# A gated state-space and GELU layer on one core: table GELU, one pool of PSUM banks and a new order of stages

## The chip, the core and the metric

The kernel runs on one core of a Trainium2 chip. The engines are TensorE (PE in the profile; PEld is its weight load), VectorE (DVE), ScalarE (ACT), GpSimd (POOL) and SyncE (SP), which issues most of the loads and stores. Matmul results land in a memory called PSUM, which these kernels use as eight banks of 512 f32 columns for each partition. The time is device time in microseconds (us). A profile of one execution has its own span, which is about 2 us shorter than that execution's time.

## The reference

Tokens are 2048, the width D is 640, the state has 640 entries, the hidden width F is 1728. For each token

```python
g = sigmoid((x * gate_w).sum(-1))
a = 2 * Re(h @ C.T) + x * Dskip      # h[t] = Lam_bar * h[t-1] + B_bar x[t], complex
b = gelu_tanh(x @ w1 + b1) @ w2 + b2
out = g * a + (1 - g) * b            # bf16
```

Both kernels turn the complex recurrence into a real one. They rotate the input by a table of cosines and sines, run a real scan with decay `r` on DVE, and rotate back. The work comes in stages over chunks of tokens: **ff1** (x times w1, then GELU), **ssm** (x times B, rotation, scan, rotation), **fin_b** (GELU output times w2, scaled by 1 - g into `gb`) and **fin_a** (states times C, plus the skip; `ot` = g times this plus `gb`, then the store).

## The kernel before

Chunks are 512, 512, 512, 384 and 128 tokens. A scheduler fixes each engine's order of instructions before the run; as the traces below show, it is not always the order of the program.

```python
CHUNKS = [512, 512, 512, 384, 128]
# start: x by a transposing DMA, then w1 in two parts (896 and 832 columns)
nc.sync.dma_start_transpose(out=xT[:, :, 0:Q], in_=x2d[0:Q, :])
nc.sync.dma_start(out=w1_sb[:, :, 0:FH], in_=B_w1[:, 0:FH].rearrange(...))
# ... (cut) tables TSIN, TCOS: seven DVE and two ACT passes per 128 states
ps1 = tile_pool(name="ps1", bufs=2, space=PSUM)   # ps_h and ps_bu: two banks each
ps2 = tile_pool(name="ps2", bufs=1, space=PSUM)   # psA and psB: two banks each, one buffer

def gelu_unit(c, kf):
    # ... (cut) five matmuls into ps_h
    nc.scalar.activation(out=xb, in_=ps_h, func=ACT.Identity, bias=b1_c)
    nc.scalar.activation(out=x2k, in_=ps_h, func=ACT.Square, bias=sb1_c, scale=SQRT_GELU_K)
    nc.scalar.activation(out=tpl, in_=x2k, func=ACT.Identity, bias=1.0)
    nc.vector.tensor_tensor(out=upl, in0=tpl, in1=xb, op=ALU.mult)
    nc.scalar.activation(out=sg, in_=upl, func=ACT.Sigmoid, scale=GELU_2C)
    nc.vector.tensor_tensor(out=gt, in0=xb, in1=sg, op=ALU.mult)

def final_B(ti):
    # ... (cut) 14 x (512 + 128) columns into psB, five gate matmuls into psB[:, 640:641]
    nc.scalar.activation(out=gcol[:, 0:1], in_=psB[:, 640:641], func=ACT.Sigmoid)
    nc.scalar.activation(out=gcol[:, 1:2], in_=psB[:, 640:641], func=ACT.Sigmoid, scale=-1.0)
    nc.scalar.activation(out=gb, in_=psB[:, 0:D], func=ACT.Identity, scale=gcol[:, 1:2])

def final_A(ti):
    # ... (cut) 10 x (512 + 128) columns and five diag matmuls into psA
    nc.vector.scalar_tensor_tensor(out=ot, in0=psA[:, 0:D], scalar=gcols[ti][:, 0:1], in1=gbs[ti], ...)
    nc.sync.dma_start(out=out2d[tcols, :], in_=ot)

# ... (cut) chunk 0, ctilde() (scales C by the input factors on DVE), then
for c in range(1, NCH):          # simplified: the last chunk differs a little
    for ks in range(KS):
        ssm_unit(c, ks)
        for kf in groups[ks]:
            gelu_unit(c, kf)
    carry_batch(c)
    for ti in tiles_of(c - 1):
        final_B(ti)
        final_A(ti)
```

Of the kernel before, what the change touches and what calls it, by code (L numbers as in the profile page):

```python
# [10 lines left out]
ALU = mybir.AluOpType  # L11
# [5 lines left out]
P = 128  # L17
T = 2048
D = 640
NS = 640  # L20
F = 1728
CH = 512
CHUNKS = [512, 512, 512, 384, 128]
NCH = len(CHUNKS)
CH_OFF = [sum(CHUNKS[:i]) for i in range(NCH)]
KD = D // P
KS = NS // P
KF = (F + P - 1) // P
F_LAST = F - (KF - 1) * P
NT = T // P  # L30

MAGIC = 12582912.0
TWO_PI_M = float(np.float32(2.0 * np.pi * (1.0 - 2.0 ** -20)))
INV_2PI = float(np.float32(1.0 / (2.0 * np.pi)))
GELU_K = 0.044715
SQRT_GELU_K = float(np.sqrt(GELU_K))
GELU_2C = float(2.0 * np.sqrt(2.0 / np.pi))
# [3 lines left out]
def kernel(  # L41
# [18 lines left out]
    dbg: dict | None = None,  # L60
):
    nc = tc.nc
    if dbg is None:
        dbg = {}

    def dbg_out(key, ap_sb):
        if key in dbg:
            nc.sync.dma_start(out=dbg[key], in_=ap_sb)

# [3 lines left out]
    const = ctx.enter_context(tc.tile_pool(name="const", bufs=1))  # L73
    hsp = ctx.enter_context(tc.tile_pool(name="hsp", bufs=2))
    gelp = ctx.enter_context(tc.tile_pool(name="gelp", bufs=2))

    xT = const.tile([P, KD, T], BF16, name="xT")
    w1_sb = const.tile([P, KD, F], BF16, name="w1_sb")
    w2_sb = const.tile([P, KF, D], BF16, name="w2_sb")
    BT_re = const.tile([P, KD, NS], BF16, name="BT_re")  # L80
    BT_im = const.tile([P, KD, NS], BF16, name="BT_im")
    CCA = const.tile([P, KS, D], BF16, name="CCA")
    CCB = const.tile([P, KS, D], BF16, name="CCB")
    TCOS = const.tile([P, KS, CH], BF16, name="TCOS")
    TSIN = const.tile([P, KS, CH], BF16, name="TSIN")

    praw = const.tile([P, 4, KS], BF16, name="praw")
    pf32 = const.tile([P, 4, KS], F32, name="pf32")
    lre_c = pf32[:, 0, :]
    lim_c = pf32[:, 1, :]  # L90
    ldt_c = pf32[:, 2, :]
    dsk_c = pf32[:, 3, :]
    b1raw = const.tile([P, KF], BF16, name="b1raw")
    b1_c = const.tile([P, KF], F32, name="b1_c")
    gw_c = const.tile([P, KD], BF16, name="gw_c")
    ident = const.tile([P, P], BF16, name="ident")
    diag = const.tile([P, KD, P], BF16, name="diag")
    tf = const.tile([P, CH], F32, name="tf")
    carry = const.tile([P, KS, 4], F32, name="carry")
    ends = const.tile([P, 2, KS], F32, name="ends")  # L100

    with nc.allow_non_contiguous_dma(reason="small parameter loads"):
        nc.scalar.dma_start(out=praw[:, 2, :], in_=A_log_dt.rearrange("(j p) -> p j", p=P))
        nc.scalar.dma_start(out=praw[:, 1, :], in_=A_Lambda_im.rearrange("(j p) -> p j", p=P))
        nc.scalar.dma_start(out=praw[:, 0, :], in_=A_Lambda_re.rearrange("(j p) -> p j", p=P))
        nc.scalar.dma_start(out=b1raw[:, 0:KF - 1], in_=B_b1[0:(KF - 1) * P].rearrange("(j p) -> p j", p=P))
        nc.scalar.dma_start(out=b1raw[:F_LAST, KF - 1:KF], in_=B_b1[(KF - 1) * P:F].rearrange("(j p) -> p j", p=F_LAST))
    Q = CH
    nc.sync.dma_start_transpose(out=xT[:, :, 0:Q], in_=x2d[0:Q, :])
    FH = 7 * P  # L110
    nc.sync.dma_start(out=w1_sb[:, :, 0:FH], in_=B_w1[:, 0:FH].rearrange("(kd p) f -> p kd f", p=P))
    nc.sync.dma_start(out=w1_sb[:, :, FH:F], in_=B_w1[:, FH:F].rearrange("(kd p) f -> p kd f", p=P))
    nc.sync.dma_start_transpose(out=BT_re[:, :, :], in_=A_B_re[:, :])  # L113
    nc.sync.dma_start_transpose(out=BT_im[:, :, :], in_=A_B_im[:, :])
    nc.sync.dma_start_transpose(out=xT[:, :, Q:2 * Q], in_=x2d[Q:2 * Q, :])

    smallp_cm = tc.tile_pool(name="smallp", bufs=1)
    smallp = smallp_cm.__enter__()

    def col(name, dtype=F32, n=KS):  # L120
        return smallp.tile([P, n], dtype, name=name)

    nc.vector.tensor_copy(out=pf32[:, 0:3, :], in_=praw[:, 0:3, :])
    nc.vector.memset(b1_c[:], 0.0)
    nc.vector.tensor_copy(out=b1_c[:, 0:KF - 1], in_=b1raw[:, 0:KF - 1])
    nc.vector.tensor_copy(out=b1_c[:F_LAST, KF - 1:KF], in_=b1raw[:F_LAST, KF - 1:KF])
# [4 lines left out]
    nc.vector.tensor_copy(out=dt32[:], in_=dt16[:])  # L131
    dtl = col("dtl")
# [3 lines left out]
    th_c = col("th_c")  # L136
    nc.vector.tensor_tensor(out=th_c[:], in0=dt32[:], in1=lim_c, op=ALU.mult)
    thp_c = const.tile([P, KS], F32, name="thp_c")
    nc.vector.tensor_scalar(out=thp_c[:], in0=th_c[:], scalar1=INV_2PI, scalar2=None, op0=ALU.mult)

    def sincos_cols(w_ap, sin_out, cos_out, tagp):
        kq = col(tagp + "_kq")
        nc.vector.tensor_scalar(out=kq[:], in0=w_ap, scalar1=MAGIC, scalar2=MAGIC, op0=ALU.add, op1=ALU.subtract)
        red = col(tagp + "_red")
        nc.vector.tensor_tensor(out=red[:], in0=w_ap, in1=kq[:], op=ALU.subtract)
        nc.scalar.activation(out=sin_out, in_=red[:], func=ACT.Sin, scale=TWO_PI_M)
        wq = col(tagp + "_wq")
        nc.vector.tensor_scalar(out=wq[:], in0=w_ap, scalar1=0.25, scalar2=None, op0=ALU.add)
        kcq = col(tagp + "_kcq")
        nc.vector.tensor_scalar(out=kcq[:], in0=wq[:], scalar1=MAGIC, scalar2=MAGIC, op0=ALU.add, op1=ALU.subtract)  # L150
        redc = col(tagp + "_redc")
        nc.vector.tensor_tensor(out=redc[:], in0=wq[:], in1=kcq[:], op=ALU.subtract)
        nc.scalar.activation(out=cos_out, in_=redc[:], func=ACT.Sin, scale=TWO_PI_M)

    sth = col("sth"); cth = col("cth")
    sincos_cols(thp_c[:], sth[:], cth[:], "t1")
    rot = {}
    for L in sorted(set(CHUNKS[:-1])):
        wL = col(f"w{L}")
        nc.vector.tensor_scalar(out=wL[:], in0=thp_c[:], scalar1=float(L), scalar2=None, op0=ALU.mult)  # L160
        sL = const.tile([P, KS], F32, name=f"s{L}")
        cL = const.tile([P, KS], F32, name=f"c{L}")
        sincos_cols(wL[:], sL[:], cL[:], f"t{L}")
        nsL = const.tile([P, KS], F32, name=f"ns{L}")
        nc.vector.tensor_scalar(out=nsL[:], in0=sL[:], scalar1=-1.0, scalar2=None, op0=ALU.mult)
        rot[L] = (cL, sL, nsL)

    a_c = col("a_c"); b_c = col("b_c")
    nc.vector.tensor_tensor(out=a_c[:], in0=r_c[:], in1=cth[:], op=ALU.mult)
    nc.vector.tensor_tensor(out=b_c[:], in0=r_c[:], in1=sth[:], op=ALU.mult)  # L170
# [8 lines left out]
    cre = col("cre"); cim = col("cim"); t2c = col("t2c")  # L179
# [5 lines left out]
    nc.vector.tensor_tensor(out=t2c[:], in0=am1[:], in1=lim_c, op=ALU.mult)  # L185
    nc.vector.tensor_tensor(out=cim[:], in0=cim[:], in1=t2c[:], op=ALU.subtract)
    nc.vector.tensor_tensor(out=cim[:], in0=cim[:], in1=rden[:], op=ALU.mult)
    c2re = const.tile([P, KS], F32, name="c2re")
    m2ci = const.tile([P, KS], F32, name="m2ci")
    m2cr = const.tile([P, KS], F32, name="m2cr")  # L190
    nc.vector.tensor_scalar(out=c2re[:], in0=cre[:], scalar1=2.0, scalar2=None, op0=ALU.mult)
    nc.vector.tensor_scalar(out=m2ci[:], in0=cim[:], scalar1=-2.0, scalar2=None, op0=ALU.mult)
    nc.vector.tensor_scalar(out=m2cr[:], in0=cre[:], scalar1=-2.0, scalar2=None, op0=ALU.mult)

    sb1_c = const.tile([P, KF], F32, name="sb1_c")
    nc.vector.tensor_scalar(out=sb1_c[:], in0=b1_c[:], scalar1=SQRT_GELU_K, scalar2=None, op0=ALU.mult)
    make_identity(nc, ident[:])
    iot = smallp.tile([P, CH], I32, name="iot")
    nc.gpsimd.iota(iot[:], pattern=[[1, CH]], base=0, channel_multiplier=0)
    nc.vector.tensor_copy(out=tf[:], in_=iot[:])  # L200
    smallp_cm.__exit__(None, None, None)

    with tc.tile_pool(name="tabw", bufs=1) as tabw:
        for ks in range(KS):
            w = tabw.tile([P, CH], F32, name="w")
            nc.vector.tensor_scalar(out=w[:], in0=tf[:], scalar1=thp_c[:, ks:ks + 1], scalar2=None, op0=ALU.mult)
            kk = tabw.tile([P, CH], F32, name="kk")
            nc.vector.tensor_scalar(out=kk[:], in0=w[:], scalar1=MAGIC, scalar2=MAGIC, op0=ALU.add, op1=ALU.subtract)
            red = tabw.tile([P, CH], F32, name="red")
            nc.vector.tensor_tensor(out=red[:], in0=w[:], in1=kk[:], op=ALU.subtract)  # L210
            nc.scalar.activation(out=TSIN[:, ks, :], in_=red[:], func=ACT.Sin, scale=TWO_PI_M)
            wq = tabw.tile([P, CH], F32, name="wq")
            nc.vector.tensor_scalar(out=wq[:], in0=w[:], scalar1=0.25, scalar2=None, op0=ALU.add)
            kc = tabw.tile([P, CH], F32, name="kc")
            nc.vector.tensor_scalar(out=kc[:], in0=wq[:], scalar1=MAGIC, scalar2=MAGIC, op0=ALU.add, op1=ALU.subtract)
            redc = tabw.tile([P, CH], F32, name="redc")
# [44 lines left out]
    def ssm_unit(c, ks):  # L261
# [14 lines left out]
        if c == 0 and ks == 0:  # L276
            dbg_out('bu16', bu16[:])
# [205 lines left out]
```

## Time and profile before

| | before |
|---|---|
| time, first measurement | 277.16 us (276.76 to 279.09) |
| span | 275.5 us |
| PE busy | 228.8 us, 83% |
| DVE busy | 215.1 us, 78% |
| ACT busy | 183.2 us, 66% |
| PE idle | 275.5 - 228.85 = 46.7 us |

These lines are from the page of the kernel before: part 1 (busy time, share, instructions) and part 2 (busy tenths in 40 slices of 6.9 us; PEclk is the granted clock in tenths).

```profile
PE 228.8 (83%) x1528; PEld 120.5 (44%) x1528; DVE 215.1 (78%) x545; ACT 183.2 (66%) x401; POOL 3.3 (1%) x12
...
PE   0357058897979888999888989998988999999994
...
DVE  0399989999999999998999989119998921699111
ACT  0369989888936788847888984139999621895111
...
PEclk9999658999999999999999999999999999999999
```

No engine is full over the span: PE has 83%, DVE 78% and ACT 66%. The next lines are from the groups of instructions by form; the columns are busy time, mean ns of one, and idle time of the engine just before, with what ended it.

```profile
L339 ACT ACTIVATE xb<-ps_h,b_c 128x512 bf16<-128x512 f32 x39 | 26.8, 687 | 1.2 <-DVE gel L349 0.7 <-PE ps_h L331 0.5
L341 ACT ACTIVATE x2k<-ps_h,sb_c 128x512 bf16<-128x512 f32 x39 | 26.7, 685 | 0.0
L344 ACT ACTIVATE tpl<-x2k 128x512 bf16<-128x512 bf16 x39 | 24.5, 629 | 0.0
...
L348 ACT ACTIVATE sg<-upl 128x512 bf16<-128x512 bf16 x39 | 23.8, 627 | 15.9 <-DVE upl L346 15.9
...
L349 DVE TENSOR_TENSOR gel<-xb,sg 128x512 bf16<-128x512 bf16 x39 | 15.8, 410 | 0.2
...
L346 DVE TENSOR_TENSOR upl<-tpl,xb 128x512 bf16<-128x512 bf16 x39 | 15.4, 405 | 1.3 <-ACT tpl L344 1.3
```

The GELU of one 128x512 unit is four ACT passes, 2.63 us in all, and two DVE passes, while its five matmuls need 5 x 0.215 us. The waits of the kernel before (in total, times, longest):

```profile
PE ps_h L331 <- ACT x2k L341: 25.8, 23, 9.5
...
PE ps_h L331 <- DMA w_sb<-in_B_w_dram: 11.3, 1, 11.3
```

The table of stages gives, for each stretch of the span, its length, the busy time of PE, PEld, DVE, ACT and POOL with the number of instructions, the granted clock, the DMA share and GB/s:

```profile
0.00:20.00 20.00, 6.58 (x18) 2.19 (x19) 8.77 (x56) 6.47 (x16) 2.20 (x9) 1.00 0.98 226
20.00:40.00 20.00, 7.85 (x29) 3.08 (x29) 18.87 (x47) 18.86 (x31) 0.00 (x0) 0.74 1.03 213
40.00:80.00 40.00, 36.12 (x163) 15.46 (x162) 40.00 (x80) 33.55 (x61) 0.00 (x0) 0.96 0.11 40
80.00:120.00 40.00, 34.15 (x229) 17.65 (x228) 40.00 (x87) 29.63 (x57) 0.00 (x0) 1.00 0.03 9
120.00:275.50 155.50, 144.14 (x1094) 82.14 (x1092) 107.50 (x279) 94.69 (x238) 1.13 (x3) 1.00 0.04 16
```

Of the 46.7 us in which PE is idle, 13.4 fall before 20 us (the first matmul waits 11.3 us for w1), 12.2 from 20 to 40 us, 9.7 from 40 to 120 us and 11.4 after. From 40 to 120 us DVE has no pause at all. At the start and after the wait of 9.5 us, PE's weight loads are 0.43 us apart (11.3 to 15.1 us and 37.8 to 41.6 us) where they are 0.22 us apart later: matmuls at half rate.

### The profile page before, as it was taken

The page shows a single profiled execution, that of the slowest core. Times are in us where ns is not written, and L with a number is a line of the kernel's source. Part 1 is how long each engine was busy: PE and PEld are TensorE (multiplying, and loading weights), DVE is VectorE, ACT ScalarE, POOL GpSimd, SP SyncE. Part 2 cuts the span into 40 slices and gives each one's busy share as a digit, 9 for nine tenths or more (in the row PEclk, how much of TensorE's full clock was granted, in tenths as well). Part 3 has the DMA queues.
Part 4 walks back from the last instruction along what each step waited for, and adds up shares of the span by engine and source line. Part 5 has one row for each costly group of instructions (what it writes and reads, how often), then busy time and mean ns, then how long its engine had stood idle before and what let it go on. Part 6 is the DMA issues. An engine that isn't in the chain of part 4 may idle for free.

```text
span 275.5 us, 4172 instructions
## 1 busy us (share of the span) xinstructions
PE 228.8 (83%) x1528; PEld 120.5 (44%) x1528; DVE 215.1 (78%) x545; ACT 183.2 (66%) x401; POOL 3.3 (1%) x12
## 2 busy tenths in 40 slices
PE   0357058897979888999888989998988999999994
PEld 0113023343434444554333445555444555766552
DVE  0399989999999999998999989119998921699111
ACT  0369989888936788847888984139999621895111
POOL 3000000000000000000000000000000000000000
PEclk9999658999999999999999999999999999999999
DMA  7999994000000000000000000100000000000000
GB/s 101 335 231 214 219 245 157 2 0 1 0 0 2 0 24 26 1 26 24 1 0 0 2 12 14 48 24 2 0 2 2 24 26 24 26 0 26 24 27 24
DMA packets 33702, 13.22 MB, mean 48 GB/s; under 512 B 28625, under 2 KB 33682, under 8 KB 33682
## 3 DMA queue, kind: packets, MB, share of 16 engines
q1 hardware_dynamic: 29954, 12.95, 18.0%
q10 hardware_dynamic: 3728, 0.01, 0.7%
q8 instruction: 12, 0.20, 0.3%
q14 instruction: 8, 0.07, 0.1%
HBM read 4.43 MB, written 2.62 MB: 26 GB/s over the span
## 4 chain that ended last, share of the span: by engine, by line
DVE 45%; PE 29%; SPq 12%; ACT 11%; DMA 1%; issue 1%; DVEq 0%; ACTq 0%
PE psB L374 11%; PE psA L399 8%; DVE upl L346 4%; DVE gel L349 4%; DVE wa L285 4%; DVE wb L286 4%; SPq L113 3%; PE psB L375 3%; ACT sg L348 3%; DVE wb L309 3%; DVE wa L308 3%; PE psA L400 2%; ACT x2k L341 2%; SPq L239 2%; ACT tpl L344 2%; PE ps_bu L268 2%
## 5 line engine op out<-in xcount | busy, mean ns | idle before, releaser
L331 PE MATMUL ps_h<-xT,w_sb 128*128 128x512 bf16 (+5 forms) x350 | 75.6, 351 | 37.9 <-ACT x2k L341 25.8
L374 PE MATMUL psB<-w_sb,gel 128*128 128x512 bf16 x224 | 66.0, 379 | 0.7 <-DVE gel L349 0.5
L331 PEld LDWEIGHTS <-w_sb 128*128 128x128 bf16 (+1 forms) x350 | 33.1, 101 | 75.7 <-issue 42.9
L348 ACT ACTIVATE sg<-upl 128x512 bf16<-128x512 bf16 (+2 forms) x70 | 37.4, 545 | 24.1 <-DVE upl L346 23.9
L375 PE MATMUL psB<-w_sb,gel 128*128 128x128 bf16 x224 | 49.0, 219 | 0.0
L339 ACT ACTIVATE xb<-ps_h,b_c 128x512 bf16<-128x512 f32 (+2 forms) x70 | 42.4, 605 | 4.3 <-PE ps_h L331 3.0
L406 DVE SCALAR_TENSOR_TENSOR ot<-psA,gcol,gb 128x640 bf16<-128x640 f32 x16 | 14.0, 875 | 37.2 <-PE psA L402 30.3
L341 ACT ACTIVATE x2k<-ps_h,sb_c 128x512 bf16<-128x512 f32 (+2 forms) x70 | 42.1, 601 | 0.0
L344 ACT ACTIVATE tpl<-x2k 128x512 bf16<-128x512 bf16 (+2 forms) x70 | 38.3, 547 | 0.1
L374 PEld LDWEIGHTS <-gel 128*128 128x128 bf16 x224 | 21.9, 98 | 24.0 <-DVE gel L349 0.8
L268 PE MATMUL ps_bu<-xT,BT_re 128*128 128x512 bf16 (+2 forms) x125 | 26.8, 338 | 2.2 <-ACT bu_674 L275 1.2
L268 PE MATMUL ps_bu<-xT,BT_im 128*128 128x512 bf16 (+2 forms) x125 | 26.2, 336 | 2.1 <-ACT bu_908 L275 1.7
L346 DVE TENSOR_TENSOR upl<-tpl,xb 128x512 bf16<-128x512 bf16 (+2 forms) x70 | 24.3, 355 | 3.2 <-ACT tpl L344 3.2
L381 ACT ACTIVATE gcol<-psB 128x1 f32<-128x1 f32 x16 | 2.8, 175 | 35.8 <-PE psB L377 35.8
L349 DVE TENSOR_TENSOR gel<-xb,sg 128x512 bf16<-128x512 bf16 (+2 forms) x70 | 24.8, 360 | 2.1 <-ACT sg L348 1.8
L399 PE MATMUL psA<-CCB,hs 128*128 128x512 bf16 x80 | 24.0, 379 | 0.0
L399 PE MATMUL psA<-CCA,hs 128*128 128x512 bf16 x80 | 23.9, 378 | 0.0
L375 PEld LDWEIGHTS <-gel 128*128 128x128 bf16 x224 | 21.9, 98 | 3.1 <-issue 0.7
L399 PEld LDWEIGHTS <-hs 128*128 128x128 bf16 x160 | 15.6, 98 | 16.5
L400 PE MATMUL psA<-CCB,hs 128*128 128x128 bf16 x80 | 17.5, 219 | 0.0
L400 PE MATMUL psA<-CCA,hs 128*128 128x128 bf16 x80 | 17.5, 219 | 0.0
L268 PEld LDWEIGHTS <-BT_im 128*128 128x128 bf16 x125 | 11.5, 98 | 13.0 <-issue 2.6
(338 smaller groups left out, 292.9 us busy)
## 6 DMA issues: line engine op xcount, KB each, us to landing
out_dram<-ot SPq DMA_DIRECT2D x16, 160.0 KB, 1.8
w_sb<-in_B_w_dram SPq DMA_DIRECT2D x1, 2080.0 KB, 8.5
w_sb<-in_B_w_dram SPq DMA_DIRECT2D x1, 1120.0 KB, 7.0
w_sb<-in_B_w_dram SPq DMA_DIRECT2D x1, 1040.0 KB, 9.0
w_sb<-in_B_w_dram SPq DMA_DIRECT2D x1, 80.0 KB, 8.2
xT<-in_A_x_dram SPq DMA_TRANSPOSE x3, 7.9
praw<-in_A_log_dt_dram ACTq DMA_DIRECT2D x1, 1.2 KB, 3.1
praw<-in_A_Lambda_im_dram ACTq DMA_DIRECT2D x1, 1.2 KB
```

The source lines that it names most:

```text
L268: nc.tensor.matmul(ps_bu[:, :L], lhsT=BT[:, kd, ks * P:(ks + 1) * P], rhs=xT[:, kd, tsl], start=(kd == 0), stop=(kd == KD - 1),)
L331: nc.tensor.matmul(ps_h[:msz, :L], lhsT=w1_sb[:, kd, kf * P:kf * P + msz], rhs=xT[:, kd, tsl], start=(kd == 0), stop=(kd == KD - 1),)
L339: nc.scalar.activation(out=xb[:msz, :L], in_=ps_h[:msz, :L], func=ACT.Identity, bias=b1_c[:msz, kf:kf + 1])
L341: nc.scalar.activation(out=x2k[:msz, :L], in_=ps_h[:msz, :L], func=ACT.Square, bias=sb1_c[:msz, kf:kf + 1], scale=SQRT_GELU_K)
L344: nc.scalar.activation(out=tpl[:msz, :L], in_=x2k[:msz, :L], func=ACT.Identity, bias=1.0)
L346: nc.vector.tensor_tensor(out=upl[:msz, :L], in0=tpl[:msz, :L], in1=xb[:msz, :L], op=ALU.mult)
L348: nc.scalar.activation(out=sg[:msz, :L], in_=upl[:msz, :L], func=ACT.Sigmoid, scale=GELU_2C)
L349: nc.vector.tensor_tensor(out=gt[:msz, kf, :L], in0=xb[:msz, :L], in1=sg[:msz, :L], op=ALU.mult)
L374: nc.tensor.matmul(psB[:, 0:512], lhsT=lhsT, rhs=w2_sb[:msz, kf, 0:512], start=(kf == 0), stop=last)
L375: nc.tensor.matmul(psB[:, 512:640], lhsT=lhsT, rhs=w2_sb[:msz, kf, 512:640], start=(kf == 0), stop=False)
L399: nc.tensor.matmul(psA[:, 0:512], lhsT=lhsT, rhs=rhs_t[:, ks, 0:512], start=(j == 0), stop=False)
L400: nc.tensor.matmul(psA[:, 512:640], lhsT=lhsT, rhs=rhs_t[:, ks, 512:640], start=(j == 0), stop=False)
```

## The change

The intent is to take ACT and DVE well below PE and then keep PE fed. The GELU becomes one ACT instruction. The scaling of C moves into a second pair of rotation tables (OCOS, OSIN). All gates are made at once, with Tanh. There are four chunks of 512, and the ff1 and ssm stages of a chunk are no longer interleaved. PSUM is one pool of eight banks. The start uses plain loads of x with PE transposes, w1 in three parts, and parameters (b1, Dskip, gate_w and others) as rows, which PE transposes to columns. The diff, cut to its core:

```diff
-CHUNKS = [512, 512, 512, 384, 128]
+NCH = T // CH
+HA = 384                       # 640 columns are cut 384 + 256, one bank each
+    ps = ctx.enter_context(tc.tile_pool(name="ps", bufs=8, space=PSUM))
-    nc.sync.dma_start_transpose(out=xT[:, :, 0:Q], in_=x2d[0:Q, :])
-    FH = 7 * P
+    nc.sync.dma_start(out=x0n[:, 0:H, :], in_=x2d[0:H * P, :].rearrange(...))
+    w1_cuts = [0, 2 * P, 7 * P, F]
+    nc.gpsimd.dma_start(out=prmB[2 * KS:2 * KS + KF - 1, :], in_=B_b1[...])
+    # ... (cut) three more rows of prmB the same way: b1's end, Dskip, gate_w
+    for _ in range(6):
+        nc.tensor.matmul(wps[:], lhsT=warm[:, 0:P], rhs=warm[:], start=True, stop=True)
+    for kd in range(KD):
+        for a in range(TPC):
+            nc.tensor.transpose(pT[:, a * P:(a + 1) * P], x0n[:, a, kd * P:(kd + 1) * P], ident[:])
+    # ... (cut) tables in three passes (the third on DVE and ACT in turn), OCOS and OSIN in four on DVE
-        # the six passes of gelu_unit
+            nc.scalar.activation(out=gel[c][:m, kf, :], in_=p[:m, :], func=ACT.Gelu_apprx_tanh,
+                                 bias=b1_c[:m, kf:kf + 1])
-            # two Sigmoids per tile
+        nc.scalar.activation(out=gz[:], in_=p[:, 0:NT], func=ACT.Tanh, scale=0.5)
+                nc.vector.scalar_tensor_tensor(out=ot[:, 0:HA], in0=p0[:, 0:HA], ...)
+                nc.vector.scalar_tensor_tensor(out=ot[:, HA:D], in0=p1[:, 0:HB], ...)
-    # the loop over chunks with ssm_unit, gelu_unit, final_B, final_A
+    ff1(0)
+    ff1(1)
+    ssm(0)
+    gates()
+    fin_b(0)
+    ssm(1)
+    fin_a(0)
+    ssm(2)
+    ff1(2)
+    fin_b(1)
+    fin_a(1)
+    # ... (cut) ssm(3), ff1(3), fin_b(2), fin_a(2), fin_b(3), fin_a(3)
```

## The prediction

> **What bounds the kernel now.** The page: span 275.5 us (timed median 277.16), PE busy 228.8, DVE 215.1, ACT 183.2; no single bound. Groups by form: each gelu unit costs ACT four passes (xb 687, x2k 685, tpl 629, sg 627 ns at 512 columns) and DVE two (405, 410 ns). The table of stages: DVE busy all of 50 to 100 us while PE has gaps; the chain of waits is 45% DVE, 29% PE, 12% SP queue. The waits list has "ps_h <- ACT x2k" at 25.8 us, the longest 9.5. That gap (28 to 37 us) also lowers the granted clock (0.50 in 30:40). PE starts only at 11.31 us, after the transposed x and half of w1, with 512-column matmuls 0.386 us apart instead of 0.215. The Trainium skill, "TensorE: Matmul & The Clock Gate", Part 1, says the array starts at half clock and falls back after about 3.4 us without work; this trace agrees at both places.
>
> **PE's floor.** Start to start in the PE timeline: 512 columns 0.215 us, the 512+128 pair 0.271, diag 0.055, gate about 0.033. ff1 280 x 0.215 = 60.2; ssm 200 x 0.215 = 43.0; fin_b 16 x 14 x 0.271 = 60.7; fin_a 16 x (10 x 0.271 + 0.275) = 47.8; gates 2.6. Total 214.3 us. The change does not lower it (384+256 is the same 640 columns).
>
> **What the change moves.**
> - Table GELU: ACT 56 passes instead of 280, DVE loses 140 (49 us). The skill, "ScalarE: Activation LUTs", says cost per element is the same for every function, so 0.6 to 0.69 us each. After: ACT about 90 us (gelu 38, bu 24, gb 14, start 14), DVE about 170 (20 ssm units of 6.5 = 130, ot 16, tables with OCOS/OSIN 19, rest 5).
> - CCA/CCB (12.4 us of DVE) go; OCOS/OSIN cost about 11, early, under ff1.
> - The 128-token chunk's small, dearer instructions go.
> - Start: plain x loads, 20 PE transposes, w1 in three cuts. I expect ff1 to begin at 7 to 8 us.
> - Order: ff1(0), ff1(1) give PE 30 us that needs no DVE while tables and loads finish. DVE then needs about 34 us per ssm chunk against 53 of PE per chunk; hs(0) ready near 76 us, fin_a(0) comes near 80. Eight banks and eight bu buffers keep PE from waiting for DVE.
>
> **Time.** Start 7.5 + floor 214.3 + cold clock at the start about 2.5 + gaps about 3 (Sin tables holding ACT while eight banks fill) + tail about 3.5 (before, 271.8 to 275.5) = 230.8; before's time is 1.7 over its span, so 232. PE idle or slow time goes; PE becomes the bound.
>
> Predicted 232 us, range 226 to 242. Chances: faster by over 2% 0.97, within 2% 0.02, slower 0.01.
>
> **What would show it.** PE busy above 93%; granted clock full from about 12 us; DVE near 170 us, ACT near 90; the chain mainly PE; first w1 matmul at 7 to 8 us; no wait of fin_a on hs over 2 us.
>
> **What would make it wrong.** Parameters on the GpSimd queue landing late and holding the first matmuls; ACT taking Sin tables ahead of gelu so that PE idles and the clock falls back (3 to 8 us); repeated table loads (1.28 us each here); hs(0) late at fin_a(0), where slack is about 4 us; the 384+256 pair costing more than 0.271 us (each 0.01 is 3.8 us).

## The result, and the profile after

| | before | after |
|---|---|---|
| time, median (range, runs) | 276.96 us (276.68 to 279.09, 4) | 237.95 us (237.33 to 238.89, 4) |
| span | 275.5 us | 235.1 us |
| PE, DVE, ACT busy | 228.8, 215.1, 183.2 us | 224.2, 170.6, 89.1 us |
| PE idle | 46.7 us | 10.9 us |

The ratio is 0.859, 95% interval 0.855 to 0.864.

The page of the kernel after, parts 1 and 2:

```profile
PE 224.2 (95%) x1436; PEld 131.8 (56%) x1436; DVE 170.6 (73%) x369; ACT 89.1 (38%) x150; POOL 5.4 (2%) x15
...
PE   6699999999999999699999999999999999999993
...
DVE  2899800499999999999999999999999503300131
ACT  2799866550335400246662220155662120022100
...
PEclk9999999999999999799999999999999999999999
```

PE now holds nines from the third slice to the end, but for the tail and one slice of 6 (94 to 100 us), with a dip of the clock in the same slice. The one GELU pass, from the groups by form:

```profile
L265 ACT ACTIVATE gel<-bank,colB 128x512 bf16<-128x512 f32 x52 | 34.4, 697 | 15.6 <-PE bank L263 15.6
```

It costs 697 ns, as much as one of the old four passes. The PE waits of the kernel after:

```profile
PE bank L275 <- DVE ot L353: 2.6, 2, 2.3
...
PE bank L157 <- DMA prmB<-in_gate_w_dram: 2.1, 1, 2.1
```

And the table of stages, in the same stretches as before:

```profile
0.00:20.00 20.00, 15.85 (x71) 7.46 (x72) 14.78 (x58) 14.05 (x24) 4.33 (x13) 1.00 0.96 245
20.00:40.00 20.00, 20.00 (x93) 8.89 (x92) 8.54 (x18) 15.18 (x25) 0.00 (x0) 1.00 1.08 263
40.00:80.00 40.00, 40.00 (x299) 23.05 (x297) 35.05 (x77) 16.59 (x31) 0.52 (x1) 1.00 0.03 6
80.00:120.00 40.00, 37.40 (x210) 20.01 (x209) 39.65 (x83) 13.80 (x23) 0.00 (x0) 0.96 0.05 17
120.00:235.10 115.10, 110.99 (x770) 72.42 (x768) 72.61 (x138) 29.47 (x52) 0.52 (x1) 1.00 0.05 18
```

PE idles 4.2 us before 20 us, not at all to 80 us, 2.6 us from 80 to 120 us and 4.1 us after, which is the tail (the time after the last matmuls). So 46.7 - 10.9 = 35.8 us of the 40.4 us that the span lost were idle time of PE; 12.2 of them lay between 20 and 40 us, where the new PE was busy 20.00 of 20.

The two gaps that remain can be read instruction by instruction. This is the PE timeline of the first 45 us (start, length, what; in brackets the idle time before and what ended it):

```profile
4.82 2.31 PE L150 MATMUL bank<-ident,x0n 128*128 128x128 bf16 x20
9.23 0.17 PE L157 MATMUL bank<-ident,prmB 24*128 24x24 bf16 x1 [2.10 <-DMA prmB<-in_gate_w_dram]
9.33 16.97 PE L263 MATMUL bank<-xT_67,w_sb 128*128 128x512 bf16 x70
26.24 15.40 PE L263 MATMUL bank<-xT_68,w_sb 128*128 128x512 bf16 x70
```

The x columns are transposed by 7.1 us. Then PE's order has the transpose of the parameter rows `prmB`, which came through the GpSimd queue, and PE waits 2.10 us for them. The 70 matmuls of ff1(0) take 16.97 us and those of ff1(1) 15.40: the difference of 1.57 us is the slow clock at the start. The weight loads show it, 0.43 us apart up to 12.2 us and 0.22 us after. The clock column reads full from the first slice on, in both kernels, although the first matmuls run at half rate; the spacing is the better witness there.

This is the timeline of all engines around the later gap:

```profile
92.10 0.44 PE L349 MATMUL bank<-diag,xT_67 128*128 128x128 bf16 x5
92.12 0.61 DVE L353 SCALAR_TENSOR_TENSOR ot<-bank,gcol,gb 128x384 bf16<-128x384 f32 x1
...
92.79 1.24 PE L275 MATMUL bank<-xT_69,BT_re 128*128 128x512 bf16 x5 [0.25 <-DVE ot L353]
...
96.81 0.59 DVE L353 SCALAR_TENSOR_TENSOR ot<-bank,gcol,gb 128x384 bf16<-128x384 f32 x1
...
97.45 1.44 PE L275 MATMUL bank<-xT_69,BT_re 128*128 128x512 bf16 x3 [2.35 <-DVE ot L353]
```

Four tiles of fin_a(0) hold all eight banks. The first tile is complete at 83.5 us, but DVE's order has its `ot` at 92.12 us, after other ssm work, and the second at 96.81. The first two groups of ssm(2) take the two banks that the first `ot` frees; the third must wait for the second `ot`. After this pause of 2.35 us the matmuls run at half rate (granted clock 0.50 from 97.45 to 100 us). That is not the same in every profile: after a pause of 2.35 us at the same place, a_dmaT and a_gatetile go on at full rate. The pause is also shorter than the 3.4 us that the prediction quotes; which pause lowers the clock stays open. The Trainium skill, "TensorE: Matmul & The Clock Gate", Part 1, "Architectural detail", says that ACT and DVE take instructions strictly in order; this trace agrees with it: the finished tile waited 8.6 us while DVE was busy with other work.

### The profile page after: what moved, and what is told of

It reads as the page before. It is cut to its first block, busy times and chain, and to the rows that moved or that the text cites. A ratio compares the mean times of both kernels' runs of the same rounds, so it can differ in the third digit from the quotient of the medians.

```text
span 235.1 us, 3571 instructions
## 1 busy us (share of the span) xinstructions
PE 224.2 (95%) x1436; PEld 131.8 (56%) x1436; DVE 170.6 (73%) x369; ACT 89.1 (38%) x150; POOL 5.4 (2%) x15
## 4 chain that ended last, share of the span: by engine, by line
PE 66%; DVE 23%; ACT 4%; DMA 2%; issue 1%; POOL 1%; DVEq 0%; POOLq 0%
PE bank L263 22%; PE bank L328 12%; PE bank L275 10%; PE bank L344 8%; DVE g L290 8%; PE bank L329 8%; PE bank L345 5%; DMA prmB<-in_gate_w_dram 2%; DVE wb L284 2%; DVE wa L283 2%; DVE wb L302 2%; DVE wa L301 2%; DVE v L285 1%; ACT TCOS L212 1%; PE bank L349 1%
## 5 line engine op out<-in xcount | busy, mean ns | idle before, releaser
L328 PE MATMUL bank<-w_sb,gel 128*128 128x384 bf16 x224 | 61.1, 326 | 0.0
L329 PE MATMUL bank<-w_sb,gel 128*128 128x256 bf16 x224 | 60.8, 272 | 0.0
L265 ACT ACTIVATE gel<-bank,colB 128x512 bf16<-128x512 f32 (+1 forms) x56 | 37.1, 696 | 17.1 <-PE bank L263 17.1
L277 ACT ACTIVATE bu<-bank 128x512 bf16<-128x512 f32 x40 | 23.9, 597 | 47.4 <-PE bank L275 47.4
L290 DVE TENSOR_TENSOR_SCAN g<-r_c,carry,v 128x512 bf16<-128x512 f32 x30 | 36.8, 1269 | 0.0
L328 PEld LDWEIGHTS <-gel 128*128 128x128 bf16 x224 | 21.8, 97 | 15.1 <-issue 0.8
L344 PE MATMUL bank<-CT_im,hs 128*128 128x384 bf16 x80 | 22.6, 326 | 0.0
L344 PE MATMUL bank<-CT_re,hs 128*128 128x384 bf16 x80 | 22.6, 326 | 0.0
L345 PE MATMUL bank<-CT_im,hs 128*128 128x256 bf16 x80 | 21.7, 273 | 0.0
L345 PE MATMUL bank<-CT_re,hs 128*128 128x256 bf16 x80 | 21.7, 272 | 0.0
L263 PE MATMUL bank<-xT_67,w_sb 128*128 128x512 bf16 (+1 forms) x70 | 16.9, 402 | 0.1
L263 PE MATMUL bank<-xT_68,w_sb 128*128 128x512 bf16 (+1 forms) x70 | 15.4, 380 | 0.0
L263 PE MATMUL bank<-xT_69,w_sb 128*128 128x512 bf16 (+1 forms) x70 | 15.4, 379 | 0.0
```

Source lines behind the costliest of these rows:

```text
L263: nc.tensor.matmul(p[:m, :], lhsT=w1_sb[:, kd, kf * P:kf * P + m], rhs=xT[c][:, kd, :], start=(kd == 0), stop=(kd == KD - 1))
L265: nc.scalar.activation(out=gel[c][:m, kf, :], in_=p[:m, :], func=ACT.Gelu_apprx_tanh, bias=b1_c[:m, kf:kf + 1])
L277: nc.scalar.activation(out=bu[:, ri, :], in_=p[:], func=ACT.Identity)
L290: nc.vector.tensor_tensor_scan(g[:, ri, :], rb, v[:, ri, :], init, ALU.mult, ALU.add)
L328: nc.tensor.matmul(p0[:, 0:HA], lhsT=lhsT, rhs=w2_sb[:m, kf, 0:HA], start=st, stop=sp)
L329: nc.tensor.matmul(p1[:, 0:HB], lhsT=lhsT, rhs=w2_sb[:m, kf, HA:D], start=st, stop=sp)
```

## The experiments

Twelve kernels were run, all with correct results and each timed beside the kernel before on one chip. The times to compare are 277 us before and 237.95 us after. The kernel after was not in the same rounds, so differences from it are comparisons across sessions, and one of under 2% is no clear verdict: the intervals of the ratios to before overlap with that of the kernel after (0.855 to 0.864) for a_gatetile and a_act_evac, and just miss it for a_oldorder, a_dmaT and a_prmB_hw.

### The old GELU in the new kernel

```diff
-            nc.scalar.activation(out=gel[c][:m, kf, :], in_=p[:m, :], func=ACT.Gelu_apprx_tanh, ...)
+            # the six passes of the kernel before: xb; then u in place by Square, Identity, x xb, Sigmoid; then xb x u
```

> The changed kernel with the old six-pass GELU put back (four ACT passes, two DVE; two of the passes in place, x0n's buffer reused for room). Theory A, the table GELU is what takes ACT and DVE under PE: ACT busy rises from 89 to about 205 us, DVE from 171 to about 220, above PE's 214 us of matmuls, so DVE bounds again and the time is 250 to 275 us; the chain is mostly DVE and ACT. Rival B, order, banks and start carry the gain and the passes would fit beside PE: within 2% of the changed kernel, 236 to 243 us.

Measured: 317.46 us (ratio to before 1.145), slower than either kernel. The table of stages:

```profile
40.00:80.00 40.00, 25.33 (x93) 9.57 (x92) 15.37 (x37) 40.00 (x74) 0.00 (x0) 0.92 0.06 15
```

Theory A had the direction right and the size too small: ACT is busy 177.8 us in all and DVE 213.9, neither near 317. Between 40 and 80 us ACT is busy 40.00 of 40 while DVE has 15.4 and PE 25.3. From 160 to 200 us it is DVE that is busy, 39.94 of 40, while ACT has 18.3 and PE 21.8. A stage of ff1 by itself is bound by ACT's four passes, a stage of ssm by DVE, and the two no longer overlap. Part of the excess is the edit's own fault: a scaled copy of b1 came late and held ACT 8.9 us. So it was run again, mended and in the old order:

```diff
-    ff1(0); ff1(1); ssm(0); ...      # stages
+    for ks in range(KS):
+        ssm(c, [ks])
+        ff1(c, groups[ks])           # units in turn, and fin_b, fin_a tile by tile
```

> a_gelu6 (the changed kernel with the old six-pass GELU) with the units of ff1 and ssm interleaved as in the kernel before, tiles of fin_b and fin_a in turn, and b1's scaled copy made early (in a_gelu6 it came late and held ACT 8.9 us). Theory A, a_gelu6's 317 us come from the new stage order: a stage of ff1 alone asks four passes of ACT, about 35 us, while PE needs 15 and DVE has little; interleaved, ACT and DVE work at the same time: 250 to 275 us. Rival B, the six passes cost that much in any order of this kernel: 300 us or more.

Measured: 284.75 us (1.030). That is 33 us better than in the new order, less the 8.9 us or so of the mended copy, and still 10 us over Theory A's range. Both theories fall in part: the new order costs the old GELU some 20 to 30 us, but banks, start, gates and tables without the table GELU, taken together, gain nothing over the kernel before either. A part of that is the gates alone, by this line of the PE timeline:

```profile
119.03 0.48 PE L345 MATMUL bank<-w_sb,gel 128*128 128x384 bf16 x1 [9.56 <-ACT gb L349]
```

Here the Tanh of all gates is done at 89.2 us, but DVE's order has the two small operations that finish them only at 117.7 us. No `gb` can leave its bank before that, and PE waits 9.56 us, with a clock of 0.70 from 108 to 125 us. What the rest would gain with other gates was not run.

### The table GELU in the old kernel

```diff
-        # xb, x2k, tpl, upl, sg, gel
+        nc.scalar.activation(out=gt[:msz, kf, :L], in_=ps_h[:msz, :L], func=ACT.Gelu_apprx_tanh, bias=b1_c[...])
```

> The kernel before with one change alone: the table GELU in place of the six passes; the gates stay two Sigmoids per tile. Theory A, GELU's passes are what the old kernel pays, but Sigmoid and the GELU table are in different sets, so each of 16 tiles loads a table twice (1.28 us each, 41 us of ACT) while the single psB waits for its eviction: 255 to 275 us. Rival B, the loads hide beside PE: as b_gelu_tanh within 1%.

The second kernel has the gate as Tanh too:

```diff
-            nc.scalar.activation(out=gcol[:, 0:1], in_=psB[:, 640:641], func=ACT.Sigmoid)   # and scale=-1.0
+            nc.scalar.activation(out=gz[:], in_=psB[:, 640:641], func=ACT.Tanh, scale=0.5)
+            # two DVE operations: 0.5 + 0.5 gz and 0.5 - 0.5 gz
```

> As b_gelu_sigm, with the gate of each tile as one Tanh and two small DVE operations, so that one table serves both. Theory A, the GELU is most of the gain: ACT falls from 183 to about 70 us, DVE from 215 to about 170, 242 to 256 us, with 3 table loads. Rival B, the new order, start and banks carry a good half: 257 us or more.

Measured: 267.60 us (0.966) with Sigmoid and 279.25 us (1.008) with Tanh. For the first, Theory A's range holds, but by luck: the Sigmoid pass loads a table 4 times and not 16, and PE has no wait for `psB` in this trace. It waits 11.4 us for w1, 11.3 us for the GELU and once 9.0 us for `psA`, until DVE reaches an `ot`. Theory A is wrong for the second: the GELU alone is not most of the gain, and the variant that was to be the better one gains nothing. ACT falls (183 to 114 and 104 us, where about 70 was expected for the second), DVE too (215 to 179 and 182), but PE stays idle: 265.2 - 227.4 = 37.8 us and 276.9 - 230.4 = 46.5 us.

Where the time stays is in the traces. ACT's timeline of the Sigmoid kernel while the tables are made:

```profile
26.77 0.69 ACT L338 ACTIVATE gel<-ps_h,b_c 128x512 bf16<-128x512 f32 x1
27.47 1.28 ACT L211 ACT_TABLE_LOAD   x1
28.77 0.63 ACT L211 ACTIVATE TSIN<-red 128x512 bf16<-128x512 f32 x1
29.30 0.61 ACT L218 ACTIVATE TCOS<-redc 128x512 bf16<-128x512 f32 x1
29.93 1.28 ACT L338 ACT_TABLE_LOAD   x1
31.23 0.69 ACT L338 ACTIVATE gel<-ps_h,b_c 128x512 bf16<-128x512 f32 x1
```

ACT goes from the table of Sin to that of GELU and back five times, 4.46 us for one GELU (26.77 to 31.23), and PE with two `ps_h` banks follows that pace (waits of 2.17 us, then five matmuls at half clock). This is an unforeseen cost of the table GELU in the old order; the Tanh kernel has it too, with 13 table loads where 3 were expected. No run changed the order of the Sin tables alone. The skill, "ScalarE: Activation LUTs", "What ACT_TABLE_LOAD costs", puts a load at about 2.7 us with its drain; here the instruction takes 1.28 us, begins as the pass before it ends (27.46 us), and the next starts at once. And the Tanh kernel has this on ACT and PE at its first long wait (timeline):

```profile
90.06 0.17 ACT L367 ACTIVATE gz<-psB 128x1 f32<-128x1 f32 x1 [2.79 <-PE psB L362]
...
102.30 0.15 DVE L368 TENSOR_SCALAR gcol<-gz 128x1 f32<-128x1 f32 x1
...
102.55 0.79 ACT L371 ACTIVATE gb<-psB,gcol 128x640 f32<-128x640 f32 x1 [12.31 <-DVE gcol L369]
...
103.39 0.58 PE L359 MATMUL psB<-w_sb,gel 128*128 128x512 bf16 x1 [10.35 <-ACT gb L371]
```

The Tanh is done at 90.2 us, but the two small DVE operations stand behind DVE's ssm work until 102.3; `psB` has one buffer, so PE waits 10.35 us and its clock falls back (0.77 from 100 to 120 us). Its waits for `psB` are 17.3 us in all, in four places. With Sigmoid that hand-over needs only ACT. With all gates made at once it happens once and not for each tile: in the kernel after, the Tanh begins at 54.6 us, DVE follows at 59.1, and PE does not stop. In a_gelu6_mix, where DVE is busy 39.3 of the 40 us from 80 to 120 us, PE waited 9.56 us at that one hand-over.

### Gates per tile in the new kernel

```diff
-    gates()
+            # in fin_b: five gate matmuls into p1[:, HB:HB + 1], two Sigmoids into gcol
```

> The changed kernel with the gates per tile again: five matmuls into the tile's second bank and two Sigmoids, no gates stage. Theory A, each tile loads an ACT table twice (about 16 x 2 x 1.28 us = 41 us of ACT), but ACT is at 38% and eight banks hide it: 236 to 241 us. Rival B, the loads sit between a tile's matmuls and the next use of its banks and cost as in the old kernel: 245 or more.

Measured: 239.32 us (0.863), 0.6% over the kernel after. Theory A holds, for a smaller reason than it gave: ACT loads 8 tables, not over 32, because the four tiles of a chunk follow each other with no GELU in between. With eight banks and no DVE in between, per-tile Sigmoid gates cost little, if anything: the intervals overlap.

### The PSUM pool

```diff
-    ps = ctx.enter_context(tc.tile_pool(name="ps", bufs=8, ...))
+    ps = ctx.enter_context(tc.tile_pool(name="ps", bufs=4, ...))
```

> The changed kernel with 4 PSUM banks instead of 8 in the one pool. Theory A, the eight banks absorb two stretches: ACT busy with Sin tables to 18.8 us while PE fills banks of ff1(0), and the ot of fin_a(0) that DVE reaches only at 92 us; with 4 banks PE waits about 4 us in the first and 6 to 9 in the second, with cold matmuls after: 246 to 254 us. Rival B, the number of banks is of no weight: 236 to 240.

Measured: 248.05 us (0.895), 10 us over the kernel after. The PE waits:

```profile
19.16 28.09 PE L263 MATMUL bank<-xT,w_sb 128*128 128x512 bf16 x120 [3.62 <-ACT gel L265]
...
98.37 0.48 PE L344 MATMUL bank<-CT_re,hs 128*128 128x384 bf16 x1 [6.21 <-DVE ot L353]
```

The two waits stand where Theory A put them, 3.62 us for the first GELU and 6.21 us for an `ot`, and both had been absorbed wholly or for the most part by the other four banks.

```diff
+    # bank() from four sets of two banks: start and ff1, ssm, fin_b, fin_a
```

> The changed kernel with the same eight PSUM banks cut into four pools of two (start and ff1, ssm, fin_b, fin_a), much as the old kernel had them. Theory A, one pool of eight is a part of the gain, as slack between engines whose order is fixed: with two banks PE waits some 6 us for the first GELU (18.8 us, behind the Sin tables) and with two for fin_a every tile after the first waits for an ot that DVE's order puts late (92 us and after): 250 to 262 us. Rival B, what counts is the number eight (4 in all gave 248) and not one pool: 237 to 242.

Measured: 254.47 us (0.918), 16.5 us over the kernel after with the same eight banks. Theory A's size holds and its first half only in part: with two banks for ff1 the scheduler drew ssm matmuls forward, and PE waits 6.41 us for BT_re from the DMA (to 19.3 us). ACT's order changed too: the first GELU runs at 12.97 us, the second, behind the Sin tables, only at 21.96. PE is busy 10.1 of the first 20 us against 15.85. When both ff1 stages and two groups of ssm(0) are done, PE is 9.0 us behind the kernel after (52.69 against 43.74 us). After that come an `ot` wait of 2.96 us and others, 7.0 us in all.

### The order before fin_a(0)

```diff
     ff1(0)
-    ff1(1)
     ssm(0)
-    gates()
-    fin_b(0)
     ssm(1)
+    ff1(1)
+    gates()
+    fin_b(0)
     fin_a(0)
```

> The changed kernel with the early stages in the old order: ff1(0), ssm(0), ssm(1), ff1(1), gates, fin_b(0), fin_a(0); from there as changed. Theory A, with 171 us of DVE against 214 of PE any order that keeps hs ahead will do: 234 to 242 us, DVE starts its first ssm unit about 28 us instead of 44. Rival B, ff1(1) ahead of ssm(0) is needed to cover tables and loads: 247 us or more, with PE waiting for DVE or for DMA before 60 us.

Measured: 239.76 us (0.867), 0.8% over the kernel after. Theory A holds: DVE starts its first ssm unit at 29.2 us in place of 44.6, and PE waits for neither DVE nor a load between the first ff1 matmul and 60 us. The gap after fin_a(0) is 4.8 us in place of 2.6. With the table GELU this part of the order is nearly free.

### The start

```diff
-    # x0n by two plain loads, 20 PE transposes, five copies
+    nc.sync.dma_start_transpose(out=xT[0][:], in_=x2d[0:CH, :])
```

> The changed kernel with the first 512 tokens of x loaded by the transposing DMA again, no PE transposes. Theory A, the plain load plus PE transposes start ff1 earlier: the first w1 matmul moves from 9.3 to 11 to 12 us and the time is 1.5 to 3 us longer (239 to 241). Rival B, the parameter columns on the GpSimd queue (they come at 9.2 us) set the start either way: no change, 237 to 238.5.

Measured: 235.95 us (0.853), 0.8% below the kernel after. Both theories fall. The first w1 matmul comes at 7.17 us, not later:

```profile
7.17 10.22 PE L254 MATMUL bank<-xT,w_sb 128*128 128x512 bf16 x40 [0.43 <-DMA w_sb<-in_B_w_dram]
18.72 22.08 PE L254 MATMUL bank<-xT,w_sb 128*128 128x512 bf16 x100 [1.33 <-ACT gel L256]
```

The transposing load of x was not what held the kernel before. That kernel waited for a first part of w1 of 896 columns; here the first part is 256 columns, and x is there by 7.2 us. The parameter rows, too, land earlier (6.57 in place of 9.23 us); why is open. Then PE waits 1.33 us, until 18.72 us, for the first GELU, which comes after the Sin tables on ACT, so only 0.84 us of the 2.2 us are left at ssm(0) (40.73 in place of 41.57). The rest of the 2 us shows after fin_a(0), where the clock did not fall in this profile (1.00 from 80 to 120 us).

```diff
-    nc.gpsimd.dma_start(out=prmB[...], ...)   # four rows
+    nc.scalar.dma_start(out=prmB[...], ...)
```

> The changed kernel with the four parameter rows of b1, Dskip and gate_w issued on the ACT queue instead of the GpSimd queue. Theory A, PE waits 2.1 us for them (7.1 to 9.2 us): the first w1 matmul moves to about 7.9 us; but the first GELU stays near 18.8 us behind the Sin tables, so the eight banks fill and PE waits there about 1 us: net 0.5 to 1.5 us shorter, 236.3 to 237.4. Rival B, the x columns or w1 hold the start: no change.

Measured: 235.81 us (0.851), 0.9% below the kernel after. The wait for `prmB` is gone. In this profile the first w1 matmul comes at 6.30 us, after ten of them PE waits 1.19 us for the next part of w1, and PE waits 1.6 us for a GELU. Theory A holds, with a gain above its range; the transposes ran at full clock in this profile (1.18 us for 18) and at half clock in that of the kernel after (2.31 us for 20), so a part of the earlier start is probably chance. best1 below has the same queue and transposes at half clock, and its first w1 matmul comes at 7.48 us.

### The gap after fin_a(0)

```diff
+                if c == 0:      # x0n is dead by now; bf16
+                    nc.scalar.activation(out=x0n[:, a, 0:HA], in_=p0[:, 0:HA], func=ACT.Identity, scale=gcol[:, 0, ti:ti + 1])
+                    nc.scalar.activation(out=x0n[:, a, HA:D], in_=p1[:, 0:HB], ...)
+                    nc.vector.tensor_tensor(out=ot[:], in0=x0n[:, a, :], in1=gbs[ti][:], op=ALU.add)
```

> The changed kernel, where the four output tiles of chunk 0 leave PSUM by ACT (scaled by the gate, bf16, into the dead x0n buffer) and DVE adds from SBUF later. Theory A, the gaps of PE at 92 to 97 us (0.25 + 2.35 us, then about 1.3 us of half-clock matmuls) come from all eight banks being held by fin_a(0) while DVE's order puts the first ot after its seventh ssm unit: the gap goes, 233 to 235.5 us. Rival B, PE waited there for the bu buffers or for DVE's work as such: same time, 237 to 239.

Measured: 237.81 us (0.858), no gain. The gap at 92 us is gone, as Theory A said, and yet the time is that of Rival B. The profile shows why: a gap of 3.42 us on an `ot`, which ends at 150.1 us, has opened after fin_a(1). The profiled run also ran its first ff1 matmuls slowly for longer (granted clock 0.59 from 10 to 15 us). This points to the right cause and too short a cure. The next kernel has it for chunks 0 to 2, with the parameter rows on the ACT queue:

> a_prmB_hw with the output tiles of chunks 0, 1 and 2 leaving PSUM by ACT (chunk 3 as it was). Theory A, in a_act_evac the gap only moved from fin_a(0) to fin_a(1) (3.4 us on an ot); with all three the gaps go and the start of a_prmB_hw stays: 231 to 234 us, PE waits on ot under 0.5 us in sum. Rival B, another wait takes its place: 235 to 237.

Measured: 231.63 us (231.52 to 232.96; ratio to before 0.837, interval 0.835 to 0.839), the fastest of all. Its page:

```profile
PE   6997999999999999999999999999999999999993
...
PEclk9999999999999999999999999999999999999999
```

Before the tail no slice is below 9 after the fourth, and the clock is full in every slice. PE's list of waits has no `ot` any more; what is left after ff1 begins is 1.4 us for the first GELU. Theory A holds, and this version beats both kernels. Its price is one more rounding to bf16 in the output; the result was correct.

## Why the prediction was right, and where not

The predicted 232 us was 6 us low, inside its range, and the mechanism was right: PE became the bound and its idle time went.

1. **Busy times.** Right: DVE 170.6 us (about 170), ACT 89.1 (about 90), PE 95% (above 93%), the chain of waits 66% PE.
2. **PE's floor, 214.3 us.** Nearly right. From the first w1 matmul (9.33 us) to the end of the last stream (230.54 + 5 x 0.055 = 230.82 us) are 221.5 us. Less 1.57 us of slow clock at the start, 2.6 us of gap and 1.7 us of slow matmuls after it (40 in 10.29 us, start to start, where 40 x 0.215 = 8.6), that is 215.6 us. The 384 + 256 pair costs 0.271 us, as assumed.
3. **"I expect ff1 to begin at 7 to 8 us."** Wrong: 9.33 us. The prediction named the GpSimd queue only as a risk; it held PE for 2.10 us, and a_prmB_hw, without that wait, is 0.9% shorter, a part of it perhaps by chance. The prediction was also wrong to list the plain loads and PE transposes among the gains: a_dmaT does without them and is no slower. What the start gained came from somewhere else; the smaller first part of w1 is likely, but no run tests it alone.
4. **"Eight banks and eight bu buffers keep PE from waiting for DVE."** Wrong at one place. PE never waited for bu (x times B, copied out of PSUM) or hs (the states), but it did for the banks of fin_a(0), 2.6 us, and the clock fell. The step counted DVE's total work per chunk and not the position of `ot` in DVE's fixed order. best1 shows it gone. The term "gaps about 3" came near to the measured 2.6 + 1.7 us by luck: it stood for Sin tables holding ACT while eight banks fill, and PE did not wait for a GELU once.
5. **The tail and the rest.** 4.3 us from the last stream to the end of the span in place of 3.5, and the profiled run's time is 2.2 us over its span in place of 1.7. By terms, the profiled run of 237.33 us lies over the sum of 232.5 (230.8 + 1.7) by 1.8 (start), 1.3 (floor), 1.3 (gaps), 0.8 (tail) and 0.5, less 0.9 for the clock at the start (1.57 in place of 2.5).

One assumption under the sum is weaker than the result suggests. The prediction costs the parts as if each took its own share off. The runs show that they do not add up:

| | all the rest old | all the rest new |
|---|---|---|
| six-pass GELU | 277 us | 317 us (285 with units interleaved) |
| table GELU | 268 us (Sigmoid), 279 us (Tanh) | 238 us |

Alone, the table GELU is worth 9 us or nothing, and the rest is worth nothing or a loss. Together they are worth 39. The GELU gives ACT and DVE room; the one pool of banks (16.5 us against the same banks cut in four) lets PE use that room. So do, by the traces and not by a run of their own, Sin tables that are finished before the first GELU and gates that need no DVE per tile. The new order works only with the short GELU; part of it (a_oldorder) hardly matters then.

Two more points are open: why the scheduler placed the first `ot` of fin_a(0) some 9 us later in DVE's order than PE needed it, and how much of the 16.5 us of a_split comes from the matmul order, which changed with the pools.

## What to carry to other kernels

When three engines are near each other in busy time, taking work from two of them shows up in the time only as far as the third is free to run ahead: look for single buffers, for table switches and for small steps on a busy in-order engine between two stages. A part that gains nothing alone may be half of a pair, so try it in both surroundings before you drop it. When a gap of PE waits for an eviction, ask where that eviction stands in its engine's order, and give it to the engine with time to spare, for every chunk and not only for the one where the gap shows.

## What the Trainium skill lacked or had wrong

- "ScalarE: Activation LUTs" puts a table load at about 2.7 us with its drain. Here each load took 1283 ns, the pass before it had just ended and the next pass began at once (27.47 to 28.77 us in b_gelu_sigm), which is the 1283 ns of "ScalarE activation tables: per-element evaluation and per-set limits" and of the first page's own figure for the load alone; its drain does not show. The first page warns of switching sets, but not that a scheduler may interleave two sets one instruction at a time, which gave 4.46 us for one GELU.
- "TensorE: Matmul & The Clock Gate", Part 4, says that the full clock "doesn't engage" for transpose mode. In a_prmB_hw 18 transposes after the warm-up matmuls took 1.18 us (weight loads 0.056 us apart), and in the kernel after 20 took 2.31 us (0.103 us apart), so a faster rate was reached there. The trace does not name the mode; the kernel calls `nc.tensor.transpose`.
- "TensorE: Matmul & The Clock Gate" warns that clock events of a trace can be unreliable; it has not this case: the granted clock reads full while the first matmuls run at half rate, 1.00 for 9.3 to 13 us in the kernel after, with weight loads 0.43 us apart.
- "Perfetto Trace Analysis" asks that all eight PSUM banks be used; it does not say what cutting them into small pools costs: 237.95 to 254.47 us here, with all eight in use.
